# Attention and a feed-forward layer on one core: a third room for the values' parts, row sums inverted on 128 rows, and new beats for a unit's work

## The chip, the cores and the metric

The kernel runs on one core of one Trainium2 chip. The metric is the device time of one execution in microseconds (us). PE is TensorE, DVE is VectorE, ACT is ScalarE, POOL is GpSimd and SP the engine that issues most of the DMAs. The runs of the kernel before took 746.44 to 747.60 us, median 746.81.

## The reference

Attention of 4 batches and 8 heads over 576 positions with head dimension 64, with a bias from a small network on the positions' distance, followed by a feed-forward layer over the 2304 tokens:

```python
scores = scale * np.matmul(q, k.transpose(0, 1, 3, 2)) + bias
scores = scores - np.max(scores, axis=-1, keepdims=True)
attn = np.exp(scores)
attn = attn / (np.sum(attn, axis=-1, keepdims=True) + 1e-09)
x = np.matmul(attn, v)                 # per head, then heads side by side: (2304, 512)
h = x @ w_in                           # (2304, 2048)
g = 0 if h <= -1, h if h >= 1, else (h + 1) ** 2 / 4
out = g @ w_out                        # (2304, 512)
```

## The kernel before

The program has three stages. The first (to about 68 us) makes the bias and writes it to DRAM. The second (about 68 to 342 us) is the attention, the third the feed-forward layer. The change lies in the second.

**Precision.** Matrix products run on values that are split in a high part (a cast to fp32r) and a low part (the value minus the high part). So each operand takes a cast and a subtraction, and each product takes two or three matmuls.

**A unit.** The attention is cut into 16 units, n = 0 to 15: a pair of heads p = n // 4 and a batch b = n % 4. The 576 query rows of two heads are five blocks of 128 rows: k = 0 to 3 hold 128 rows of either head (j = 0, 1), and "L" holds the last 64 rows of both. The steps of a unit have short names:

- S0 to S3, SL (`score`, matmuls of L431 into tiles S): scores in PSUM, in the two rooms of pool `psS`. A block takes both rooms, so the next block starts when the maxima before it have read their room.
- m00 to m31, mL (`maxima`, L457 on DVE): adds the bias, writes the tile e to SBUF and the row's extreme to mx.
- x00 to x31, xL (`exps`, L454 on ACT): the exponential, in place, with the row sum into a column of `sum` (128 x 9).
- T00 to T31, TL, Ts0, Ts1 (`transpose...`, L434 on PE): e transposed into PSUM tiles T, in the four rooms of pool `psT`, which the output tiles O share. Ts1 also transposes `sum` into 9 x 128 of its tile.
- h.. and l.. (`high`, `low_`): split the transposed tile into hi and lo. For four keys in the set POOL, ACT copies the tile to SBUF (L533, tile c) and POOL makes hi (L541) and lo (L542). For the others ACT casts hi (L536) and DVE subtracts for lo (L544).
- O00h, O00l, ... O11l (`values`, L431, tiles O): hi and lo times the values' tile vs. c00 to c11 (L569 on ACT) copy the result out, and `store` sends it to DRAM (L577 on SP).
- R (`sums_out`): ACT adds 1e-9 to the transposed sums and writes r, 9 x 128 (L548). r (`inverse`): DVE inverts it (L552) and SP stores it in rT (L553). The feed-forward stage multiplies by it.
- kh, kl0, kl1, vh, vl: the split of the next unit's inputs. kh (L171) casts queries and keys on DVE, vh (L179) casts the values into the front half of vs on DVE, and POOL subtracts for the back halves (L147). vs has two rooms, so vh of unit n+1 must wait until the last matmul on vs of unit n-1, O11l.

**The order.** Nothing is scheduled at run time: every engine takes its instructions in program order. The table BEAT gives each step of a unit a time in us from its S0, and units lie UNIT = 15.5 apart. All events of all units are sorted by that time and written out in that order. A unit's last steps (beats over 15.5) so fall into the next unit. XQ and WQ put extra work into some units: the split of the feed-forward stage's first inputs x (units 4, 8, 12 to 15) and of its first weights (units 6, 7, 9, 10).

Of the kernel before, what the change touches and what calls it, by code (L numbers as in the profile page):

```python
# [8 lines left out]
F32 = mybir.dt.float32  # L9
F32R = mybir.dt.float32r  # L10
I32 = mybir.dt.int32
U16 = mybir.dt.uint16
AF = mybir.ActivationFunctionType
ALU = mybir.AluOpType
# [7 lines left out]
P = 128  # L22
NP = H // 2
HS = S // 2
NG = S // 16
# [4 lines left out]

CBW = (1, 1, 32, C, C, C * H, S // 4, NG)
CB = sum(CBW)
CFG = dict(un=[('paaa', 'paav')[g in (1, 30, 32, 34)] for g in range(NG)], bb=5, mv=1, rb='a', pool=((0, 0), (0, 1), (1, 1), (2, 0)), sb=4, keep=1, drain=2, diag='a', rb2='v', eps='v', rc=2, rbb=1, hb=2, rawb=(2, 2), eb=4, seq=0, pb=(6, 9, 12, 14, 16), pq=22, tb=6, ub=12, low0='ppp', anch=(8, 8, 16, 23, 23), low1='ppp', ob=4, gb=4, fin=2, sbf=('v', 'v', 'v', 'v', 'v'), bsE=(), ytail='p')
EPS = 1e-9
RB = 2
FIRST = ((0, 3), (1, 5), (2, 33))
XQ = {(0, 0): (39, "raw", 4, 12.4), (1, 0): (80, "raw", 8, 12.4), (2, 0): (118, "raw", 12, 12.4), (3, 0): (139, "bias", 15, 6.3),
      (0, 1): (125, "x", 13, 12.4), (1, 1): (131, "raw", 14, 12.4), (2, 1): (144, "x", 15, 9.7), (3, 1): (151, "raw", 15, 12.4)}
WQ = {(0, 0): (52, 6), (0, 1): (70, 7), (1, 0): (91, 9), (1, 1): (100, 10)}
LB = ((1, 1), (2, 1), (3, 2), (3, 3), (2, 3))  # L40
UNIT = 15.5
BEAT = {
# [10 lines left out]
}  # L53
POOL, SB, KEEP, RBB = CFG["pool"], CFG["sb"], CFG["keep"], CFG["rbb"]
BIG = 3.0e38
# [4 lines left out]
def attn_cpb_moe_kernel(ctx, tc, qk, vL, cb, win, wout, lw, ident, ii, out):  # L60
    nc = tc.nc
# [16 lines left out]
    wp0 = ctx.enter_context(tc.tile_pool(name="m_w0", bufs=1))  # L78
    rps = [ctx.enter_context(tc.tile_pool(name="m_raw", bufs=1))]
    loads = ExitStack()  # L80
    lp = ctx.enter_context(tc.tile_pool(name="a_load", side="right", bufs=2))
    bp = loads.enter_context(tc.tile_pool(name="a_bias", side="right", bufs=CFG["bb"]))
    qp = loads.enter_context(tc.tile_pool(name="a_qkv", side="right", bufs=2))
# [4 lines left out]
    last_y, stored = [], []  # L88
    half_s = wp0.tile([P, 1], F32, name="half_s")
    nc.gpsimd.memset(half_s, 0.5)  # L90
    eps_s = wp0.tile([P, 1], F32, name="eps_s")
    nc.gpsimd.memset(eps_s, EPS)
    floor_s = wp0.tile([P, 1], F32, name="floor_s")
    nc.gpsimd.memset(floor_s, -4095.5 / 8192)

# [44 lines left out]
    qkv, bias = {}, {}  # L140
    go = [False]

    def low(o, i, h, x="p"):
        if x == "v":
            nc.vector.tensor_tensor(out=o, in0=i, in1=h.bitcast(F32), op=ALU.subtract)
            return
        pool(nc.gpsimd.tensor_tensor(out=o, in0=i, in1=h.bitcast(F32), op=ALU.subtract))  # L147

    def keep(ins):
        tc.keep_in_program_order(ins)  # L150
# [9 lines left out]
    def prep(n):  # L160

        L = CFG["low0"] if n == 0 else CFG["low1"] if n == 1 else "ppp"
        a = qkv[n] = {}

        def high(ins):
            keep(ins)

        def high_k():

            a["h"] = qp.tile([P, KQ], F32R, tag="kh", name=f"kh{n}", bufs=CFG["hb"])  # L170
            high(nc.vector.tensor_copy(a["h"], a["r"]))  # L171

        def load_r():
            a["r"] = lp.tile([P, KQ], F32, tag="qk", name=f"qk{n}", bufs=CFG["rawb"][0])
            nc.sync.dma_start(out=a["r"], in_=qk[n])

        def high_v():
            a["v"] = qp.tile([P, 10, P], F32R, tag="vs", name=f"vs{n}")
            high(nc.vector.tensor_copy(a["v"][:, :, 0:D], a["rv"]))  # L179

        def load_v():
            a["rv"] = lp.tile([P, 10, D], F32, tag="v", name=f"v{n}", bufs=CFG["rawb"][1])
            nc.sync.dma_start(out=a["rv"].rearrange("p a b -> p (a b)"), in_=vL[n])

        def part(i):


            def f():
                if i == 0:
                    a["l"] = qp.tile([P, KQ], F32R, tag="kl", name=f"ls{n}")  # L190
                c = slice(KW * i, KW * i + (QW if i else KW))
                low(a["l"][:, c], a["r"][:, c], a["h"][:, c], L[i])

            return f

        def v_():
            low(a["v"][:, :, D:P], a["rv"], a["v"][:, :, 0:D], L[2])

        return [load_r, load_v, high_k, high_v, part(0), part(1), v_]

    preps = {0: prep(0), 1: prep(1)}


    with ExitStack() as ph:
# [21 lines left out]
        diag = [ac.tile([P, P], F32, name=f"diag{i}") for i in range(2)]  # L226
# [9 lines left out]
        pq = cp.tile([P, 2, C, H], F32, name="pq")  # L236
# [148 lines left out]
    def split_x(k, j, home):  # L385

        r, rr = load_x(0, k, j, home)
        x = r[:, 0]

        def add():  # L390
            keep(nc.vector.tensor_tensor(out=x, in0=x, in1=r[:, 1], op=ALU.add))

        def scaled():
            keep(nc.vector.tensor_tensor(out=x, in0=x, in1=rr, op=ALU.mult))

        def high():
            xs[k, j] = [x_tile(j, k, i, f"x{'hl'[i]}0_{k}_{j}") for i in range(2)]
            keep(nc.scalar.copy(xs[k, j][0], x))

        def rest():  # L400
            h, l = xs[k, j]
            pool(nc.gpsimd.tensor_tensor(out=l, in0=x, in1=h.bitcast(F32), op=ALU.subtract))

        return add, scaled, high, rest

    with ExitStack() as ph:
# [3 lines left out]
        sp = ph.enter_context(tc.tile_pool(name="a_small", bufs=2))  # L410
# [32 lines left out]
        def on(n, t, f, *a):  # L443
            events.append((UNIT * n + t, len(events), f, a))

        def unit(n):
            p, b = n // B, n % B
            q = qkv[n]
            e, sc, tr, out, mx = {}, {}, {}, {}, {}
            eT = {}  # L450
            sm = stp.tile([P, 9], F32, tag="sum", name=f"sum{n}", bufs=3)
# [86 lines left out]
            def low_(key):  # L538
# [4 lines left out]
                else:  # L543
                    keep(nc.vector.tensor_tensor(out=lo, in0=ps, in1=hi.bitcast(F32), op=ALU.subtract))  # L544

            def sums_out():
                r = out["r"] = sp.tile([9, P], F32, tag="r", name=f"r{n}")
                keep(nc.scalar.activation(r, out["sum"], AF.Identity, bias=eps_s[:9]))  # L548

            def inverse():  # L550
                r = out["r"]
                keep(nc.vector.reciprocal(out=r, in_=r))  # L552
                nc.sync.dma_start(out=rT[p][b].rearrange("(k q) -> k q", q=P), in_=r)  # L553

            def values(half, j, part):
# [43 lines left out]
            for x in ("L", "s0", "s1"):  # L599
                at(f"h{x}", high, x)  # L600
                at(f"l{x}", low_, x)
            at("R", sums_out)
            at("r", inverse)
            for half in range(2):
# [20 lines left out]
                on(B * (p - 1) + b, 3.1 * k_ + 0.5, load_b)  # L625

        def plan_x(k, j):
            T, home, n, t = XQ[k, j]
            fs = []

            def load():
                assert all((k, t_) in made for t_ in range(TH * j, TH * j + TH))
                fs.extend(split_x(k, j, home))

            on(T // 10, T % 10 * UNIT / 10, load)
            for i, dt in enumerate((0, 0.9, 2.4, 3.4)):
                on(n, t + dt, lambda i=i: fs[i]())

        for kj in XQ:
            plan_x(*kj)  # L640
        for fo, (T, n) in WQ.items():
            load, *fs = weight_ahead(*fo, rps[0])
            on(T // 10, T % 10 * UNIT / 10, load)
            for t, f in zip((7.0, 9.3, 12.4, 13.3, 15.8), fs):
                on(n, t, f)
        go[0] = True
        while events:
            i = min(range(len(events)), key=lambda i: events[i][:2])
            _, _, f, a = events.pop(i)
# [5 lines left out]
    with ExitStack() as ph:  # L655
# [220 lines left out]
        for k in range(2):  # L876
            t = T1 + 1 + 12 * k
# [17 lines left out]
        for blk in (0, TB):  # L895
            for m in range(2 * NF):
                f, j = m // 2, m % 2
# [50 lines left out]
        for g in range(NG2):  # L948
            blk, f = b2, 2 * g
            for s_ in range(NS):  # L950
                t = NS * g + s_
# [30 lines left out]
                else:  # L982
                    fo, j = {2: (f, 0), 4: (f + 1, 1), 5: (f + 1, 0), 6: (f, 1)}[s_]
# [80 lines left out]
```

## Time and profile before

| | |
|---|---|
| median of the runs | 746.81 us |
| the profiled execution | 745.66 us, its span 743.5 us |
| PE busy | 704.1 us, 95% of the span |
| DVE, ACT, POOL busy | 513.3, 513.6 and 512.3 us, 69% each |
| mean granted TensorE clock | 0.993 of full speed |

A busy share of PE is not a measure of its work: matmuls overlap, and their ends are modelled. What PE loses is read from the starts of its instructions. The engines' waits name what released them. Times in the rows count from the span's start.

### The profile page before, as it was taken

The page shows a single profiled execution, that of the slowest core. Times are in us where ns is not written, and L with a number is a line of the kernel's source. Part 1 is how long each engine was busy: PE and PEld are TensorE (multiplying, and loading weights), DVE is VectorE, ACT ScalarE, POOL GpSimd, SP SyncE. Part 2 cuts the span into 40 slices and gives each one's busy share as a digit, 9 for nine tenths or more (in the row PEclk, how much of TensorE's full clock was granted, in tenths as well). Part 3 has the DMA queues.
Part 4 walks back from the last instruction along what each step waited for, and adds up shares of the span by engine and source line. Part 5 has one row for each costly group of instructions (what it writes and reads, how often), then busy time and mean ns, then how long its engine had stood idle before and what let it go on. Part 6 is the DMA issues. An engine that isn't in the chain of part 4 may idle for free.

```text
span 743.5 us, 14025 instructions
## 1 busy us (share of the span) xinstructions
PE 704.1 (95%) x4864; PEld 603.9 (81%) x4864; DVE 513.3 (69%) x993; ACT 513.6 (69%) x1124; POOL 512.3 (69%) x445
## 2 busy tenths in 40 slices
PE   5777999999999999999999999999999999999997
PEld 2234888888888888888989889898999988888896
DVE  7998767778887877896876766354455556666653
ACT  8996887889989888796565656444534447666563
POOL 7984777787887878885667677466555645666652
PEclk9998999999999999999999999999999999999999
DMA  6788334633753454326445554132021002000002
GB/s 191 237 283 254 113 118 151 199 131 114 221 158 124 145 177 128 87 70 191 130 161 163 188 151 143 45 92 78 1 64 33 1 1 85 1 2 1 0 1 85
DMA packets 51237, 83.97 MB, mean 113 GB/s; under 512 B 11216, under 2 KB 31456, under 8 KB 51168
## 3 DMA queue, kind: packets, MB, share of 16 engines
q1 hardware_dynamic: 50880, 82.87, 35.8%
q8 instruction: 38, 0.62, 0.4%
q14 instruction: 31, 0.25, 0.1%
q10 hardware_dynamic: 288, 0.22, 0.1%
HBM read 57.95 MB, written 25.12 MB: 112 GB/s over the span
## 4 chain that ended last, share of the span: by engine, by line
PE 55%; ACT 10%; DVE 8%; POOL 7%; issue 6%; DMA 4%; SPq 1%; DVEq 0%; POOLq 0%; ACTq 0%
PE y L672 23%; PE h L672 15%; PE p L672 7%; PE O L431 4%; PE S L431 3%; POOL lo L542 3%; ACT e L454 2%; DVE e L457 2%; PE T L434 2%; ACT hi L536 2%; POOL ls L147 2%; POOL hi L541 1%; DMA bias<-bias_d 1%; DVE r L552 1%; DMA x<-rT 1%
## 5 line engine op out<-in xcount | busy, mean ns | idle before, releaser
L914 POOL TENSOR_TENSOR gl<-c,gh 128x384 fp32r<-128x384 f32 x64 | 70.6, 1103 | 101.9 <-issue 87.3
L454 ACT ACTIVATE e<-e,mx 128x576 f32<-128x576 f32 x128 | 99.1, 775 | 36.3 <-DVE mx L457 36.0
L672 PE MATMUL y<-w1h,gl 128*128 128x512 f32 x288 | 114.0, 396 | 0.0
L672 PE MATMUL y<-w1l,gh 128*128 128x512 f32 x288 | 113.7, 395 | 0.0
L672 PE MATMUL y<-w1h,gh 128*128 128x512 f32 x288 | 112.0, 389 | 0.0
L457 DVE CUSTOM_DVE_ANT_0 e<-S,bias 128x576 f32<-128x576 f32 x128 | 90.8, 744 | 8.5 <-PE S L431 5.6
L542 POOL TENSOR_TENSOR lo<-c,hi 128x512 fp32r<-128x512 f32 x64 | 83.6, 1307 | 5.1
L541 POOL CAST hi<-c 128x512 fp32r<-128x512 f32 x64 | 48.4, 757 | 56.1 <-ACT c L533 56.1
L732 ACT ACTIVATE c<-c,half_s 128x384 f32<-128x384 f32 x64 | 39.4, 616 | 61.6 <-DVE c L729 61.5
L434 PE MATMUL T<-id_s,e 128*128 128x128 f32 x512 | 74.4, 279 | 0.0
L938 POOL TENSOR_TENSOR gl<-c,gh 128x384 fp32r<-128x384 f32 x32 | 32.7, 1023 | 47.8 <-issue 22.3
L434 PEld LDWEIGHTS T<-id_s,e 128*128 128x128 f32 x512 | 59.3, 144 | 6.5 <-issue 3.2
L672 PEld LDWEIGHTS y<-w1h,gl 128*128 128x128 f32 x288 | 54.0, 187 | 11.5
L672 PEld LDWEIGHTS y<-w1l,gh 128*128 128x128 f32 x288 | 54.0, 187 | 8.0
L270 ACT ACTIVATE u<-lw,nthr 128x576 f16<-128x576 f32 (+17 forms) x104 | 57.5, 644 | 4.2 <-DVE lw L235 2.4
L672 PEld LDWEIGHTS y<-w1h,gh 128*128 128x128 f32 x288 | 54.1, 188 | 7.7
L431 PE MATMUL O<-hi,vs 128*128 128x256 f32 (+1 forms) x320 | 58.5, 313 | 0.0
L289 PEld LDWEIGHTS <-qh 128*32 128x32 f16 x704 | 19.5, 101 | 47.7 <-issue 23.0
L272 POOL TENSOR_SCALAR u<-lw,thr 128x576 f16<-128x576 f32 (+17 forms) x36 | 51.7, 1453 | 7.6 <-DVE lw L235 3.9
L431 PE MATMUL S<-kh 64*128 64x288 f32 x256 | 53.3, 349 | 3.7 <-DVE mx L457 2.2
L431 PE MATMUL O<-lo,vs 128*128 128x256 f32 (+1 forms) x320 | 54.4, 300 | 0.0
L910 ACT CAST gh<-c 128x384 fp32r<-128x384 f32 x64 | 32.8, 513 | 30.3 <-DVE c L735 28.5
(263 smaller groups left out, 2043.9 us busy)
## 6 DMA issues: line engine op xcount, KB each, us to landing
bias_d<-y SPq DMA_DIRECT2D x36, 295.5 KB, 5.0
qk<-in_qk_dram SPq DMA_DIRECT2D x16, 640.0 KB, 4.1
x<-xT SPq DMA_DIRECT2D x48, 192.0 KB, 3.4
raw<-in_win_dram SPq DMA_DIRECT2D x16, 512.0 KB, 4.5
raw<-in_wout_dram SPq DMA_DIRECT2D x16, 512.0 KB, 3.5
v<-in_vL_dram SPq DMA_DIRECT2D x16, 320.0 KB, 5.5
bias<-bias_d SPq DMA_DIRECT2D x16, 288.0 KB, 3.7
out_dram<-o SPq DMA_DIRECT2D x17, 256.0 KB, 2.1
```

The source lines that it names most:

```text
L270: tc.keep_in_program_order(nc.scalar.activation(u[:, :n_], lw1[:, :n_], AF.Sigmoid, bias=nthr[:, m : m + 1], scale=STEEP))
L272: EN[x].tensor_scalar(out=u[:, :n_], in0=lw1[:, :n_], scalar1=thr[:, m : m + 1], scalar2=None, op0=ALU.is_gt)
L431: keep(nc.tensor.matmul(*a, **k))
L434: keep(nc.tensor.transpose(*a))
L454: keep(nc.scalar.activation(ev, ev, AF.Exp, bias=m, scale=-1.0, accum_out=sm[:, at : at + 1]))
L457: keep(nc.vector.tensor_tensor_reduce(out=o.rearrange("p (a b) -> p a b", a=2), in0=ps[:, :, :HS], in1=of.rearrange("p (a b) -> p a b", a= ...
L541: keep(nc.gpsimd.tensor_copy(hi, ps))
L542: keep(nc.gpsimd.tensor_tensor(out=lo, in0=ps, in1=hi.bitcast(F32), op=ALU.subtract))
L672: a = nc.tensor.matmul(out, w, x, start=start, stop=stop)
L732: keep(nc.scalar.activation(c, c, AF.Square, scale=0.5, bias=half_s))
L910: keep(nc.scalar.copy(gh, c))
L914: keep(nc.gpsimd.tensor_tensor(out=gl, in0=c, in1=gh.bitcast(F32), op=ALU.subtract))
```

## The change

Four things are changed.

1. The tile vs gets three rooms instead of two.
2. The row sums are inverted before the transposition. DVE adds 1e-9 to `sum` (128 x 9) and inverts it there; Ts1 transposes the inverses, and ACT only copies them out to r, from where SP stores them.
3. In the set POOL the key (1,1) is replaced by (3,1), so l11 is now made by DVE and the parts of (3,1) by POOL.
4. The table of beats is new, and so are some places of the extra work. Weights now fall into units 6, 7, 10 and 11.

```diff
-CFG = dict(..., pool=((0, 0), (0, 1), (1, 1), (2, 0)), ...)
+CFG = dict(..., pool=((0, 0), (0, 1), (2, 0), (3, 1)), ...)
...
-WQ = {(0, 0): (52, 6), (0, 1): (70, 7), (1, 0): (91, 9), (1, 1): (100, 10)}
+WQ = {(0, 0): (53, 6), (0, 1): (70, 7), (1, 0): (93, 10), (1, 1): (110, 11)}
...
-    "h30": 14.3, "O00l": 14.5, "l21": 14.8, "T31": 15.1, "xL": 15.3, "l30": 15.4, "diag": 16.1, "c00": 16.6,
+    "T30": 15.07, "xL": 15.09, "c00": 15.89, "r": 15.97, "diag": 16.17, "h31": 16.68, "TL": 16.69,
...
-            a["v"] = qp.tile([P, 10, P], F32R, tag="vs", name=f"vs{n}")
+            a["v"] = qp.tile([P, 10, P], F32R, tag="vs", name=f"vs{n}", bufs=3)
...
+            def inverse():
+                keep(nc.vector.tensor_scalar(out=sm, in0=sm, scalar1=EPS, scalar2=None, op0=ALU.add))
+                keep(nc.vector.reciprocal(out=sm, in_=sm))
+
             def sums_out():
-                r = out["r"] = sp.tile([9, P], F32, tag="r", name=f"r{n}")
-                keep(nc.scalar.activation(r, out["sum"], AF.Identity, bias=eps_s[:9]))
-
-            def inverse():
-                r = out["r"]
-                keep(nc.vector.reciprocal(out=r, in_=r))
+                r = sp.tile([9, P], F32, tag="r", name=f"r{n}")
+                keep(nc.scalar.copy(r, out["sum"]))
                 nc.sync.dma_start(out=rT[p][b].rearrange("(k q) -> k q", q=P), in_=r)
...
-            for t, f in zip((7.0, 9.3, 12.4, 13.3, 15.8), fs):
+            for t, f in zip((6.85, 11.0, 13.1, 15.4, 17.9), fs):
                 on(n, t, f)
```

What this does to the order is seen at two places. The first is DVE in the middle of unit 10. In a name such as lo10_0_4125 the first number is the unit and the next the half or block; the last is a buffer. T10_1_1 is the transposed tile of step T11, S10_3_0 the scores of S3 for head 0, vs11 the values' tile of the next unit. Before:

```order
L544 TENSOR_TENSOR lo9_1_3985<-T9_s1_4113,hi9_1_3984 128x320
L171 CAST kh11_4147<-qk11_3866 128x1280
L552 RECIPROCAL r9_4138<-r9_4138 9x128
L457 ISA e10_2_4150,mx10_2_4149<-S10_2_0_4151,bias2_2_3373 128x576
L457 ISA mx10_2_4149 128x1
L457 ISA e10_2_4150,mx10_2_4149<-S10_2_1_4152,bias2_2_3373 128x576
L457 ISA mx10_2_4149 128x1
L544 TENSOR_TENSOR lo10_0_4125<-T10_1_0_4171,hi10_0_4124 128x4x128
L179 CAST vs11_4220<-v11_4070 128x10x64
L457 ISA e10_3_4201,mx10_3_4200<-S10_3_0_4202,bias2_3_3434 128x576
L457 ISA mx10_3_4200 128x1
L457 ISA e10_3_4201,mx10_3_4200<-S10_3_1_4203,bias2_3_3434 128x576
```

The same stretch after:

```order
L544 TENSOR_TENSOR lo9_1_3981<-T9_s1_4113,hi9_1_3980 128x320
L171 CAST kh11_4149<-qk11_3873 128x1280
L457 ISA e10_2_4153,mx10_2_4152<-S10_2_0_4154,bias2_2_3380 128x576
L457 ISA mx10_2_4152 128x1
L457 ISA e10_2_4153,mx10_2_4152<-S10_2_1_4155,bias2_2_3380 128x576
L457 ISA mx10_2_4152 128x1
L544 TENSOR_TENSOR lo10_0_4126<-T10_1_0_4171,hi10_0_4125 128x4x128
L179 CAST vs11_4218<-v11_4071 128x10x64
L544 TENSOR_TENSOR lo10_0_4126<-T10_1_1_4187,hi10_0_4125 128x4x128
L457 ISA e10_3_4201,mx10_3_4200<-S10_3_0_4202,bias2_3_3437 128x576
L457 ISA mx10_3_4200 128x1
L544 TENSOR_TENSOR lo10_0_4126<-T10_s0_4196,hi10_0_4125 128x256
```

The inversion of r is gone from ahead of m20; the cast of vs11 keeps its place behind l10, but l11 now stands between it and m30, and ls0 between m30 and m31. The inversion now stands ahead of the next unit's m00, behind l21 (and, in this unit, a weight's cast):

```order
L544 TENSOR_TENSOR lo10_1_4242<-T10_2_1_4253,hi10_1_4241 128x4x128
L132 CAST w0h1_1483<-a10_4234 128x512
L547 TENSOR_SCALAR sum10_4039<-sum10_4039 128x9
L548 RECIPROCAL sum10_4039<-sum10_4039 128x9
L457 ISA e11_0_4304,mx11_0_4303<-S11_0_0_4305,bias2_0_2804 128x576
```

The second place is ACT where the sums of unit 9 leave the transposed tile T9_s1, with the semaphores that an instruction waits for. Before:

```order
L536 CAST hi9_1_3984<-T9_s1_4113 128x320 [waits PE_49]
L454 ACTIVATE e10_1_4089,sum10_4039<-e10_1_4089,mx10_1_4088 128x576 [waits DVE_49]
L548 ACTIVATE r9_4138<-T9_s1_4113,eps_s_113 9x128 [waits DMAHW5_49]
L454 ACTIVATE e10_1_4089,sum10_4039<-e10_1_4089,mx10_1_4088 128x576 [waits DVE_49]
L533 COPY c4_4166<-T10_0_0_4119 128x512 [waits PE_49,Pool_49]
```

After:

```order
L536 CAST hi9_1_3980<-T9_s1_4113 128x320 [waits PE_49]
L454 ACTIVATE e10_1_4091,sum10_4039<-e10_1_4091,mx10_1_4090 128x576 [waits DVE_49]
L552 COPY r9_4146<-T9_s1_4113 9x128 [waits DMAHW5_49,DVE_49]
L454 ACTIVATE e10_1_4091,sum10_4039<-e10_1_4091,mx10_1_4090 128x576
L116 ACTIVATE raw10_3871<-raw10_3871,floor_s_113 128x512 [waits DMAHW1_49]
```

The step stands where it stood, but now it waits for DVE (for ls1, which reads the same tile and is written ahead of it); before, ls1 was written behind it and waited for it.

## Rows read from the trace of the kernel before

**Rows 1.** The page: span; busy us, share of the span and instructions by engine.
```profile
span 743.5 us, 14025 instructions
...
PE 704.1 (95%) x4864; PEld 603.9 (81%) x4864; DVE 513.3 (69%) x993; ACT 513.6 (69%) x1124; POOL 512.3 (69%) x445
```
**Rows 2.** Windows: stretch, length; busy PE, PEld, DVE, ACT, POOL; clock, DMA share, GB/s.
```profile
220.00:260.00 40.00, 38.82 (x335) 34.22 (x334) 32.48 (x72) 36.63 (x92) 31.98 (x28) 1.00 0.43 137
260.00:300.00 40.00, 38.04 (x317) 33.09 (x316) 29.88 (x70) 32.87 (x84) 32.22 (x29) 1.00 0.47 143
460.00:500.00 40.00, 40.00 (x201) 36.07 (x200) 18.22 (x29) 17.11 (x31) 24.34 (x21) 1.00 0.18 58
```
**Rows 3.** Waits, 100 to 335 us: who waited for whom, total us, times, longest.
```profile
DVE vs L179 <- PE O L431: 28.6, 13, 2.2
ACT e L454 <- DVE mx L457: 27.5, 23, 2.0
```
**Rows 4.** Timeline of PE: start us, us, what, [idle before]; SL of unit 0.
```profile
80.09 0.40 PE L431 MATMUL S_L<-kh 128*128 128x288 f32 x1
```
**Rows 5.** Timeline of PE around SL of units 6, 7 and 15; S1, S2, S3 of unit 7.
```profile
179.33 1.04 PE L434 MATMUL T<-id_s,e 128*128 128x128 f32 x8
180.84 0.37 PE L431 MATMUL S_L<-kh 128*128 128x288 f32 x1 [0.48 <-DVE mx L457]
...
181.86 0.63 PE L434 MATMUL T<-id_s,e 128*128 128x128 f32 x4
...
186.81 0.40 PE L431 MATMUL S<-kh 64*128 64x288 f32 x2
...
187.81 0.44 PE L434 MATMUL T_s<-id_s,e 128*128 128x128 f32 x2
...
191.07 0.66 PE L434 MATMUL T<-id_s,e 128*128 128x128 f32 x4
...
193.04 0.86 PE L431 MATMUL S<-kh 64*128 64x288 f32 x2
...
194.49 1.00 PE L431 MATMUL O<-hi,vs 128*128 128x320 f32 x5
...
196.06 1.03 PE L434 MATMUL T<-id_s,e 128*128 128x128 f32 x8
197.58 0.37 PE L431 MATMUL S_L<-kh 128*128 128x288 f32 x1 [0.48 <-DVE mx L457]
...
331.71 1.04 PE L434 MATMUL T<-id_s,e 128*128 128x128 f32 x8
332.50 0.38 PE L431 MATMUL S_L<-kh 128*128 128x288 f32 x1
...
333.38 0.60 PE L434 MATMUL T<-id_s,e 128*128 128x128 f32 x4
```
**Rows 6.** Timeline of DVE in unit 7: ls1 of unit 6, inversion, m20, l10, vh.
```profile
190.08 0.49 DVE L544 TENSOR_TENSOR lo<-T_s,hi 128x320 fp32r<-128x320 f32 x1 [0.72 <-ACT r L548]
...
191.22 0.93 DVE L552 RECIPROCAL r<-r 9x128 f32<-9x128 f32 x1
192.08 0.68 DVE L457 CUSTOM_DVE_ANT_0 e<-S,bias 128x576 f32<-128x576 f32 x1
...
193.38 0.67 DVE L544 TENSOR_TENSOR lo<-T,hi 128x512 fp32r<-128x512 f32 x1
196.26 0.49 DVE L179 CAST vs<-v 128x640 fp32r<-128x640 f32 x1 [2.21 <-PE O L431]
```
**Rows 7.** Timeline of POOL in unit 15.
```profile
332.02 1.29 POOL L542 TENSOR_TENSOR lo<-c,hi 128x512 fp32r<-128x512 f32 x1
```
**Rows 8.** Timeline of DVE in units 0 and 15.
```profile
78.69 0.67 DVE L179 CAST vs<-v 128x640 fp32r<-128x640 f32 x1
...
329.63 0.54 DVE L391 TENSOR_TENSOR x<-x 128x384 f32<-128x384 f32 x1
...
332.40 1.32 DVE L391 TENSOR_TENSOR x<-x 128x384 f32<-128x384 f32 x1
```

More of the change, by code (lines that the diff above doesn't have):

```diff
@@ L32 @@
 CB = sum(CBW)
-CFG = dict(un=[('paaa', 'paav')[g in (1, 30, 32, 34)] for g in range(NG)], bb=5, mv=1, rb='a', pool=((0, 0), (0, 1), (1, 1), (2, 0)), sb=4, keep=1, drain=2, diag='a', rb2='v', eps='v', rc=2, rbb=1, hb=2, rawb=(2, 2), eb=4, seq=0, pb=(6, 9, 12, 14, 16), pq=22, tb=6, ub=12, low0='ppp', anch=(8, 8, 16, 23, 23), low1='ppp', ob=4, gb=4, fin=2, sbf=('v', 'v', 'v', 'v', 'v'), bsE=(), ytail='p')
+CFG = dict(un=[('paaa', 'paav')[g in (1, 30, 32, 34)] for g in range(NG)], bb=5, mv=1, rb='a', pool=((0, 0), (0, 1), (2, 0), (3, 1)), sb=4, keep=1, drain=2, diag='a', rb2='v', eps='v', rc=2, rbb=1, hb=2, rawb=(2, 2), eb=4, seq=0, pb=(6, 9, 12, 14, 16), pq=22, tb=6, ub=12, low0='ppp', anch=(8, 8, 16, 23, 23), low1='ppp', ob=4, gb=4, fin=2, sbf=('v', 'v', 'v', 'v', 'v'), bsE=(), ytail='p')
 EPS = 1e-9
@@ L36 @@
 FIRST = ((0, 3), (1, 5), (2, 33))
-XQ = {(0, 0): (39, "raw", 4, 12.4), (1, 0): (80, "raw", 8, 12.4), (2, 0): (118, "raw", 12, 12.4), (3, 0): (139, "bias", 15, 6.3),
-      (0, 1): (125, "x", 13, 12.4), (1, 1): (131, "raw", 14, 12.4), (2, 1): (144, "x", 15, 9.7), (3, 1): (151, "raw", 15, 12.4)}
-WQ = {(0, 0): (52, 6), (0, 1): (70, 7), (1, 0): (91, 9), (1, 1): (100, 10)}
+USUAL = (10.0, 13.1, 14.05, 17.9)
+XQ = {(0, 0): (39, "raw", 4, USUAL), (1, 0): (80, "raw", 8, USUAL), (2, 0): (120, "raw", 12, USUAL), (3, 0): (140, "bias", 15, (6.1, 6.2, 8.0, 8.1)),
+      (0, 1): (125, "x", 13, USUAL), (1, 1): (133, "raw", 14, USUAL), (2, 1): (144, "x", 15, (9.5, 10.0, 10.9, 11.1)), (3, 1): (153, "raw", 15, (13.1, 13.2, 14.5, 16.3))}
+WQ = {(0, 0): (53, 6), (0, 1): (70, 7), (1, 0): (93, 10), (1, 1): (110, 11)}
 LB = ((1, 1), (2, 1), (3, 2), (3, 3), (2, 3))
@@ L90, in attn_cpb_moe_kernel @@
     nc.gpsimd.memset(half_s, 0.5)
-    eps_s = wp0.tile([P, 1], F32, name="eps_s")
-    nc.gpsimd.memset(eps_s, EPS)
     floor_s = wp0.tile([P, 1], F32, name="floor_s")
@@ L627, in plan_x @@
         def plan_x(k, j):
-            T, home, n, t = XQ[k, j]
+            T, home, n, ts = XQ[k, j]
             fs = []
@@ L635, in plan_x @@
             on(T // 10, T % 10 * UNIT / 10, load)
-            for i, dt in enumerate((0, 0.9, 2.4, 3.4)):
-                on(n, t + dt, lambda i=i: fs[i]())
+            for i, t in enumerate(ts):
+                on(n, t, lambda i=i: fs[i]())
         for kj in XQ:
```

19 rows, old and new, of the table BEAT are left out of this document.

## The prediction, written before the result was known

> **What bounds the kernel now.** I read the page first, then the windows, then PE's timeline inside a unit, then DVE's. The page gives PE as busy for 95% of the span [rows 1], which says little by itself. The windows divide the kernel: in the feed-forward stage PE is busy for all of 40.00 us [rows 2], and nothing of that stage's own work is changed. So the attention is what can move. There PE's busy time is 38.04 to 38.82 us of 40, with every other engine below 37 [rows 2].
>
> How much PE loses is read from its starts. SL of unit 0 starts at 80.09 and SL of unit 15 at 332.50 [rows 4, 5]: 252.41 us for 15 units. A plain unit takes 197.58 - 180.84 = 16.74 us [rows 5]. Fifteen of those are 251.1; the other 1.3 us I put down to units that carry extra work.
>
> Two stalls lie in each unit. The first is before SL: in unit 6 eight transposes start at 179.33 and SL follows at 180.84, 1.51 us later; in unit 15, where SL does not wait, the same step takes 332.50 - 331.71 = 0.79. That is 0.72, and SL itself then takes 1.02 (to 181.86) against 0.88 (to 333.38), 0.14 more [rows 5]. The second is in S3: it takes 194.49 - 193.04 = 1.45 us, S1 takes 1.00 [rows 5], so 0.45. Together 1.31 us per unit. Without them PE needs 16.74 - 1.31 = 15.43 us for a unit.
>
> DVE shows where the stalls come from. Vh of the next unit waits 2.21 us for PE's last O matmul, and only then m30 runs, for which SL waits [rows 6]. This is one of 13 such waits, 28.6 us in total; ACT's waits for maxima, 27.5 us, are the shadow of it [rows 3]. Earlier in the unit ls1 waits 0.72 us for ACT's r, and the inversion takes 0.93 right before m20 [rows 6]; S3 waits for m20 and m21.
>
> **The third room.** With three rooms, vh of unit n+1 takes the room of unit n-2, whose last reader lies a whole unit back. The 2.21 us go. What is late next for SL? From S3's end PE has O11h and O11l (196.06 - 194.49 = 1.57) and eight transposes (0.79), so 2.36 us to SL's start, in another order but the same work [rows 5]. In that time DVE must finish m30. It starts it when S3 is done, if vh and l11 are done by then. Counted from S2's end (191.07): m20 and m21 are 1.36, l10 0.67, vh 0.49, l11 0.67, so 3.19 us; S3 ends 2.97 us after S2's end (1.97 to its start, 1.00 to run) [rows 5, 6]. So m30 starts about 0.3 us after S3 and takes 0.68: SL's need is met some 1.4 us early. l11 also needs ACT's cast of T11, which stands behind an exponential and an output copy; that may cost some tenths of the 1.4 us, not all.
>
> **The inversion.** Ahead of m20 the inversion (0.93) and ls1's wait (0.72) go, and m20 starts when S2 ends. PE has 193.04 - 191.07 = 1.97 us from S2's end to S3's start [rows 5]; m20 and m21 take 1.36 [rows 6]. S3 does not wait, by 0.6 us. The price: two operations on 128 x 9 on DVE, not in the trace; the inversion of 9 x 128 bounds them at 0.93 each from above [rows 6], nothing from below; with an eighth or less of the free elements I take 0.1 each. They stand ahead of the next unit's m00 and wait for the last exponential on ACT, which is the new coupling: behind them are m00, m01 and so S1. SL to the end of the next S0 is about 4 us of PE work, mL and the exponential after it need under 2, so I cost the wait at nothing; if ACT is late by more than that cover, it is paid in full at S1.
>
> ACT's copy of r now waits for DVE's ls1, at most its 0.49 us [rows 6]. Queued behind it on ACT are x11 and the copies of T00 and T01, which POOL waits for. The other direction of this wait cost DVE 0.72; ACT has the time as long as it is not the bound.
>
> **The other engines at 15.4 us a unit.** From 260 to 300 us ACT is busy 32.87 of 40, 13.7 us of a unit of 16.74; from 220 to 260, with two weights in it, 36.63, or 15.3 [rows 2]. POOL's 32.22 make 13.5, DVE's 32.48 make 13.6. So all fit in 15.4, ACT in units with a weight only just. Moving (1,1) to DVE and (3,1) to POOL changes no engine's count. I allow 0.2 us in each of the four units with a weight.
>
> **DMAs.** Their share is 0.43 and 0.47 [rows 2] and grows by 8%. Stores and loads keep their queue; the store of r comes from ACT's copy rather than DVE's inversion, about a microsecond earlier. Nothing of this is costed.
>
> **The sum.** PE's floor is 15.43; for the transposes that now stand apart I take 15.5. 15 x 15.5 = 232.5, plus 1.3 for the extra work as before, plus 4 x 0.2: 234.6 against 252.41, a gain of 17.8 us. PE's order up to SL of unit 0 is the same, and after SL of unit 15 PE runs its tail and the saturated stage with the same work: nothing there, with 1 us either way. The profiled execution took 745.66 and gives 727.9; the median of the runs lies 1.15 above it (746.81), so I expect **729.0 us**. The least: fifteen units at 15.43 and nothing for weights or extra work, a gain of 21 us, 726.
>
> **Rival 1: POOL holds vh up.** In unit 15 DVE's addition at 332.40 takes 1.32 us, the same at 329.63 takes 0.54; POOL's subtraction runs from 332.02 to 333.31, and the addition ends 0.41 us after that [rows 7, 8]. So DVE is held until POOL's instruction is done. In unit 0 vh takes 0.67 rather than 0.49 [rows 6, 8]. In the new order vh stands where POOL works through l00, kl0 and kl1 without a pause, and the wait could reach a POOL instruction's 1.29. Vh, l11 and m30 then slip by that: it eats 1.1 to 1.4 us of cover. With l11's wait for ACT on top some 0.4 us per unit come out at SL: 6 us, 735. The Trainium skill states this as a rule ("SBUF — State Buffer", section "SBUF: two separate sides"): VectorE and GpSimd share a pair of ports, an exclusive lock that is held for a whole instruction, while the other blocks; the rows above agree, and by that rule the place of vh beside POOL's back-to-back work is the weak point of this change.
>
> **Rival 2: SL's wait only changes its cause.** m30 now stands behind l11, which waits for ACT's cast behind x20 and c10. If ACT runs late by 1.4 us, SL waits 0.86 as before, and only S3's 0.45 and its like are won: 17.8 - 15 x 0.86 = 4.9, 742.
>
> **Rival 3, slower: ACT becomes the bound.** ACT has 13.7 us of work and now three waits in a unit in which all that follows is queued: r for DVE, the last exponential's maximum, the first one's. If these add up to over 3.0 us, a unit takes more than 16.74. At 3.4 us, 15 x 0.4 = 6 us lost: 753. Against it: ACT's waits for maxima came to 27.5 us over 14 units, 2 us each [rows 3], and their main cause goes.
>
> **Rival 4: it doesn't do what it says.** A DMA (the values' load, which waits for POOL's part of vs) takes the place of the room as what vh waits for, and the period stays near 16.7: 746. The DMA shares speak against it.
>
> **How the numbers follow.** Forecast (725.5 to 733) 0.63; rival 1, 0.15; rival 2, 0.07; rival 3, 0.08; rival 4, 0.04; below 725.5, 0.03. The range is 725.5 to 738: from the floor to beyond rival 1, with some of what lies between it and rival 2. Left out are rivals 2 to 4 and the lower end, 0.2. A change of 0.2% (1.5 us) is about what a measurement of this kernel can tell from none: faster 0.63 + 0.15 + 0.07 + 0.03 = 0.88, the same 0.04, slower 0.08.
>
> **What would show it.** In the profile after, SL to SL should be 15.4 to 15.6 us, with no idle time named DVE mx before SL; the wait of vs for O should be gone, ls1 should follow m11 without one. PE's 252.41 us from SL of unit 0 to SL of unit 15 should be about 235, and what follows SL of unit 15 as long as before (411 us to the span's end). Rival 1 shows as vh taking 1 us and more and SL waiting for mx; rival 2 as DVE's lo waiting for ACT's hi before m30; rival 3 as ACT without idle time and m00 late behind the inversion. The prediction is wrong if the period stays over 16.2.

## The result, and the profile after

The changed kernel takes 736.66 us (734.78 to 736.93), the kernel before beside it 747.2 us: a ratio of 0.985, 95% interval 0.983 to 0.987. It is faster by 10.5 us. That is inside the predicted range, but the forecast of 729.0 us promised 17.8, and its own band (725.5 to 733) was missed. The profiled execution took 736.86 us.

The page of the changed kernel, span and busy time, answers [rows 1]: PE's busy time falls by 9 us with the span, DVE's grows by 17.

```profile
span 734.5 us, 14012 instructions
...
PE 695.0 (95%) x4864; PEld 600.4 (82%) x4864; DVE 530.4 (72%) x1009; ACT 512.4 (70%) x1124; POOL 514.0 (70%) x444
```

The windows, for [rows 2] (length; PE, PEld, DVE, ACT, POOL; clock, DMA share, GB/s):

```profile
220.00:260.00 40.00, 40.00 (x360) 36.64 (x360) 34.10 (x79) 38.36 (x98) 35.56 (x31) 1.00 0.49 150
260.00:300.00 40.00, 37.27 (x322) 32.54 (x319) 37.10 (x71) 33.66 (x86) 32.37 (x29) 1.00 0.44 134
460.00:500.00 40.00, 40.00 (x201) 36.11 (x201) 19.20 (x30) 16.94 (x31) 23.24 (x20) 1.00 0.23 75
```

From 220 to 260 us PE is now without a gap in the attention, as in the saturated stage. From 260 to 300 it is worse off than before (37.27 against 38.04), and there DVE's 37.10 is 7.2 us more than before. So the change did in one stretch what was forecast and in another the opposite.

The waits, 100 to 335 us, for [rows 3]: the wait of vs for O is gone, ACT's wait for maxima has fallen from 27.5 to 10.5 us.

```profile
ACT e L454 <- DVE mx L457: 10.5, 16, 1.1
```

The timeline of PE answers [rows 4, 5]: start, duration, what, idle before it. SL of units 0, 4, 5, 6, 7 and 15, and in between what waits in unit 4 (T21 before SL, the two first matmuls of S1 of unit 5 after it).

```profile
80.11 0.40 PE L431 MATMUL S_L<-kh 128*128 128x288 f32 x1 [0.97 <-DVE mx L457]
...
141.56 0.63 PE L434 MATMUL T<-id_s,e 128*128 128x128 f32 x4 [0.18 <-DVE lo L544]
142.14 0.40 PE L431 MATMUL S_L<-kh 128*128 128x288 f32 x1
...
148.90 0.40 PE L431 MATMUL S<-kh 64*128 64x288 f32 x1 [0.61 <-DVE mx L457]
149.58 0.40 PE L431 MATMUL S<-kh 64*128 64x288 f32 x1 [0.28 <-DVE mx L457]
...
159.16 0.38 PE L431 MATMUL S_L<-kh 128*128 128x288 f32 x1
...
174.53 0.38 PE L431 MATMUL S_L<-kh 128*128 128x288 f32 x1
...
189.88 0.38 PE L431 MATMUL S_L<-kh 128*128 128x288 f32 x1
...
322.45 0.40 PE L431 MATMUL S_L<-kh 128*128 128x288 f32 x1
```

A plain unit takes 174.53 - 159.16 = 15.37 us, and 189.88 - 174.53 = 15.35 with a weight in it, against 16.74 before. But from SL of unit 4 to SL of unit 5 it is 159.16 - 142.14 = 17.02. From SL of unit 0 to SL of unit 15 it is 242.34 us (before 252.41). Fifteen units at 15.36 would be 230.4: 11.9 us lie elsewhere. They lie around units 4, 8 and 12 to 15 alone: 2.2, 2.5 and 7.2 us. These are the units in which DVE does the x work, the part of the extra work that adds the two halves of a block of the attention's result (x, line 391) and scales it by the inverted sums (line 394). There are eight such blocks.

The timeline of DVE in unit 3 (the first line, a plain place) and unit 4:

```profile
129.08 1.27 DVE L547 TENSOR_SCALAR sum<-sum 128x9 f32<-128x9 f32 x1
...
138.29 0.69 DVE L179 CAST vs<-v 128x640 fp32r<-128x640 f32 x1
138.91 1.91 DVE L391 TENSOR_TENSOR x<-x 128x384 f32<-128x384 f32 x1
140.74 0.68 DVE L544 TENSOR_TENSOR lo<-T,hi 128x512 fp32r<-128x512 f32 x1
...
143.02 1.56 DVE L394 TENSOR_TENSOR x<-x,xr 128x384 f32<-128x384 f32 x1
...
146.41 1.57 DVE L547 TENSOR_SCALAR sum<-sum 128x9 f32<-128x9 f32 x1
148.01 0.22 DVE L548 RECIPROCAL sum<-sum 128x9 f32<-128x9 f32 x1
```

The timeline of POOL beside it:

```profile
138.59 3.64 POOL L147 TENSOR_TENSOR ls<-qk,kh 128x640 fp32r<-128x640 f32 x2
...
142.87 1.29 POOL L542 TENSOR_TENSOR lo<-c,hi 128x512 fp32r<-128x512 f32 x1
...
146.38 1.57 POOL L147 TENSOR_TENSOR vs<-v,vs 128x640 fp32r<-128x640 f32 x1
```

Read the two together. The addition to x took 0.54 us where it stood free [rows 8]; here it takes 1.91 and starts 0.32 us into POOL's work on kl. The scale starts 0.15 us into POOL's lo and takes 1.56. The 1e-9 on 128 x 9, nine elements a row, starts 0.03 us into POOL's vl and takes 1.57 us. T21 then waits for l11, which stands behind the addition (140.74, done at 141.42), and S1 waits for the maxima behind the inversion. In plain units the 1e-9 takes 1.27 us as well, and PE doesn't notice: unit 1 lasts 15.37 us with 1.27, unit 2 15.35 with 0.17.

One wait of PE for maxima is left before SL, in unit 0 (the first line of PE's timeline): 0.97 us. There the cast vh stands beside POOL's kl and takes 1.57 us:

```profile
77.22 1.57 DVE L179 CAST vs<-v 128x640 fp32r<-128x640 f32 x1
```

```profile
76.87 3.31 POOL L147 TENSOR_TENSOR ls<-qk,kh 128x640 fp32r<-128x640 f32 x2
```

SL of unit 0 starts at 80.11 all the same, against 80.09 before.

The costs over the attention (60 to 345 us), DVE grouped by line (count, busy us, mean ns, idle before):

```profile
L547 DVE TENSOR_SCALAR sum<-sum 128x9 f32<-128x9 f32 x16 | 14.2, 886 | 1.1 <-ACT e_L L454 0.3
...
L391 DVE TENSOR_TENSOR x<-x 128x384 f32<-128x384 f32 x8 | 11.9, 1483 | 0.0
L179 DVE CAST vs<-v 128x640 fp32r<-128x640 f32 x15 | 11.8, 789 | 0.0
...
L394 DVE TENSOR_TENSOR x<-x,xr 128x384 f32<-128x384 f32 x5 | 7.7, 1546 | 0.0
```

In the kernel before, the addition had a mean of 705 ns, the scale (these five) of 931. The same work costs 2.1 and 1.7 times as much.

My theory then, A: DVE's operations from SBUF to SBUF are held while POOL's instruction runs, and the new beats put the x work beside POOL's kl and lo, where PE has no cover left. The rivals: it is the amount of the x work (B); the third room or the new inversion, not the beats, makes what gain there is (told apart by doing each alone).

### The profile page after: what moved, and what is told of

It reads as the page before. It is cut to its first block, busy times and chain, and to the rows that moved or that the text cites. A ratio compares the mean times of both kernels' runs of the same rounds, so it can differ in the third digit from the quotient of the medians.

```text
span 734.5 us, 14012 instructions
## 1 busy us (share of the span) xinstructions
PE 695.0 (95%) x4864; PEld 600.4 (82%) x4864; DVE 530.4 (72%) x1009; ACT 512.4 (70%) x1124; POOL 514.0 (70%) x444
## 4 chain that ended last, share of the span: by engine, by line
PE 60%; DVE 11%; POOL 6%; ACT 5%; issue 4%; DMA 3%; SPq 2%; DVEq 0%; POOLq 0%; ACTq 0%
PE y L672 21%; PE h L672 13%; PE p L672 7%; PE O L431 6%; PE S L431 5%; PE T L434 4%; DVE e L457 3%; POOL lo L542 2%; DMA x<-rT 1%; DVE x L394 1%; DVE lo L544 1%; SPq L377 1%; DVE sum L547 1%; PE T_s L434 1%; PE S_L L431 1%
## 5 line engine op out<-in xcount | busy, mean ns | idle before, releaser
L542 POOL TENSOR_TENSOR lo<-c,hi 128x512 fp32r<-128x512 f32 x64 | 85.2, 1331 | 5.1
L541 POOL CAST hi<-c 128x512 fp32r<-128x512 f32 x64 | 44.1, 689 | 43.0 <-ACT c L533 42.9
L431 PE MATMUL O<-hi,vs 128*128 128x256 f32 (+1 forms) x320 | 57.0, 308 | 0.3 <-ACT x L569 0.3
L431 PE MATMUL S<-kh 64*128 64x288 f32 x256 | 49.4, 346 | 6.5 <-DVE mx L457 5.6
L729 DVE TENSOR_SCALAR c<-h 128x384 f32<-128x384 f32 x64 | 35.4, 552 | 27.2 <-PE h L672 25.4
```

The source lines that it names most:

```text
L431: keep(nc.tensor.matmul(*a, **k))
L541: keep(nc.gpsimd.tensor_copy(hi, ps))
L542: keep(nc.gpsimd.tensor_tensor(out=lo, in0=ps, in1=hi.bitcast(F32), op=ALU.subtract))
L729: keep(nc.vector.tensor_scalar(out=c, in0=h, scalar1=-1.0, scalar2=1.0, op0=ALU.max, op1=ALU.min))
```

## The experiments

**The third room alone.** The kernel before with one edit.

```diff
-            a["v"] = qp.tile([P, 10, P], F32R, tag="vs", name=f"vs{n}")
+            a["v"] = qp.tile([P, 10, P], F32R, tag="vs", name=f"vs{n}", bufs=3)
```

> The kernel before with the third room for vs alone. Theory (the stall before SL comes from the cast of the values waiting for PE, the stall in S3 from the inversion and from ls1's wait): the 0.86 us before SL go in every unit, the 0.45 us in S3 stay, so a plain unit takes 15.9 us instead of 16.74 and the time is about 747 - 13 = 734 us. Rival (the room alone does nothing with the old beats, since m30 then waits for something else): a plain unit of 16.5 us or more, 744 us or more.

Measured: 731.67 us, ratio 0.980 (0.976 to 0.985). All units take 15.78 to 15.87 us, those with x work too; only the last takes 16.05. One line of the change does at least as well as the whole: the two intervals of the ratio overlap a little, but the fifteen units take 237.55 us against 242.34. What is left of the stalls shows in PE's timeline of this kernel, around S3 of unit 8:

```profile
202.91 0.86 PE L431 MATMUL S<-kh 64*128 64x288 f32 x2
...
204.36 0.99 PE L431 MATMUL O<-hi,vs 128*128 128x320 f32 x5
...
205.92 1.04 PE L434 MATMUL T<-id_s,e 128*128 128x128 f32 x8
206.71 0.38 PE L431 MATMUL S_L<-kh 128*128 128x288 f32 x1
```

S3 still takes 204.36 - 202.91 = 1.45 us, to the hundredth what it took before [rows 5]; eight transposes to SL take 206.71 - 205.92 = 0.79, what they take without a wait. So the room took away the stall before SL (0.86) and left the one in S3 (0.45). And vh is held by POOL here:

```profile
L179 DVE CAST vs<-v 128x640 fp32r<-128x640 f32 x15 | 18.0, 1202 | 0.0
```

1.20 us in the mean, against 0.51 before, and SL does not wait for it. The scale of x takes 1.53 to 1.54 us in five units here, as long as in the changed kernel, and these units are no longer than the others. So an operation that is held need not cost anything; that hangs on what stands behind it.

**All of the change but the third room.**

```diff
-            a["v"] = qp.tile([P, 10, P], F32R, tag="vs", name=f"vs{n}", bufs=3)
+            a["v"] = qp.tile([P, 10, P], F32R, tag="vs", name=f"vs{n}")
```

> The changed kernel with two rooms for vs. Theory: the cast of vs waits for O11l again, and l11 and m30 stand behind it; O11l's end to m30's end is then 0.1 + 0.5 + 0.7 + 0.7 = 2.0 us, of which PE covers 0.4 with T21: a stall of 1.6 us before SL, a plain unit of 17.0 instead of 15.36 us, 737 + 24 = 761 us. Rival (the beats do it, the room is a detail): a plain unit under 15.7 us, under 742 us.

Measured: 769.43 us, ratio 1.031 (1.028 to 1.034), units of 17.05 to 17.3 us up to the first x work, as expected (17.0), then of 17.8 to 19.5, and 16.2 for the last. The direction is as expected and the size larger; where the rest comes from was not followed. The new beats are no use without the room.

**The new inversion without the 1e-9** (that addition is left out; a row's sum is far above it).

```diff
-                keep(nc.vector.tensor_scalar(out=sm, in0=sm, scalar1=EPS, scalar2=None, op0=ALU.add))
```

> The changed kernel without the addition of 1e-9 to the row sums (left out; the inversion stays). Theory A (the addition, SBUF to SBUF on DVE, is held 1.3 to 1.5 us by POOL's subtraction for vs, and the inversion is not of that kind): the inversion runs at once in about 0.2 us, m00 comes over 1 us earlier in the units with x work, and the 0.9 us before and in S1 go in five of them: about 732 us. Theory B (POOL holds whichever of the two comes first): the inversion takes 1.5 us instead, and the time stays at 736 to 737 us.

Measured: 732.76 us, ratio 0.982 (0.979 to 0.985); SL of unit 0 to SL of unit 15 237.68 us, 4.7 less than with it. Plain units stay at 15.36; units with x work take 15.8 to 16.9. DVE's timeline of this kernel, the inversion alone:

```profile
289.27 0.21 DVE L547 RECIPROCAL sum<-sum 128x9 f32<-128x9 f32 x1
```

And POOL's at that time:

```profile
289.20 1.56 POOL L147 TENSOR_TENSOR vs<-v,vs 128x640 fp32r<-128x640 f32 x1
```

The same 128 x 9 elements, at the same place in the order, beside the same instruction of POOL: the addition of a constant was held for 1.51 us in the changed kernel (1.57 in unit 4), the inversion is not held at all. So theory A is too wide as it stands: not every operation from SBUF to SBUF is held. Why the one is and the other isn't, no run here shows.

**The changed kernel without DVE's x work** (the addition and the scale of the eight blocks are left out).

```diff
-            keep(nc.vector.tensor_tensor(out=x, in0=x, in1=r[:, 1], op=ALU.add))
+            pass
...
-            keep(nc.vector.tensor_tensor(out=x, in0=x, in1=rr, op=ALU.mult))
+            pass
```

> The changed kernel without the two DVE operations (addition and scaling) on the eight blocks of x in the attention (left out; loads, ACT's cast and POOL's subtraction stay). Theory A (these two, with two SBUF operands, are held by POOL and push m30, m31, mL and the inversion): the units with x work fall from 15.9 to 17.6 us to about 15.4, and the 242.3 us from SL of unit 0 to SL of unit 15 to about 231: 726 us. Theory B (the later units are held by POOL's own extra subtraction or by a DMA for x): less than half of it goes, over 731 us.

Measured: 724.4 us, ratio 0.971 (0.968 to 0.973), 231.46 us for the fifteen units, or 15.43 each. The x work is what 10.9 of the 11.9 us are tied to. The rest lies in the same units (15.43 to 15.73 us), where POOL still makes the low part of x and the 1e-9 takes 0.97 to 1.27 us. The run does not say yet whether it is the amount of the x work or its place.

**The x work elsewhere.** Nothing is left out. POOL sat idle from 133.76 to 136.66 us in the changed kernel, some 7.5 us after SL; the addition and the scale of five blocks go there, for three of them one unit later, and the loads of two weights, which use the same room, follow. In `XQ` a block has the time of its load, its room, its unit, and the beats of its four steps (addition, scale, high part on ACT, low part on POOL). Three of the blocks (QUIET) have ACT's and POOL's steps moved as well, two (LATE) only DVE's.

```diff
-USUAL = (10.0, 13.1, 14.05, 17.9)
-XQ = {(0, 0): (39, "raw", 4, USUAL), (1, 0): (80, "raw", 8, USUAL), (2, 0): (120, "raw", 12, USUAL), ...
-      (0, 1): (125, "x", 13, USUAL), (1, 1): (133, "raw", 14, USUAL), ...
+QUIET, LATE = (6.1, 6.2, 8.0, 8.1), (6.1, 6.2, 14.05, 17.9)
+XQ = {(0, 0): (39, "raw", 5, QUIET), (1, 0): (80, "raw", 9, QUIET), (2, 0): (120, "raw", 13, QUIET), ...
+      (0, 1): (125, "x", 13, LATE), (1, 1): (137, "raw", 14, LATE), ...
```

> The changed kernel with nothing left out; the add and the scale of five of the eight x blocks are put some 6 beats after a unit's first scores, where GpSimd sits idle in the trace of the changed kernel (2.9 us of it at 133.8 us), three of the blocks one unit later for it. Theory A (these operations cost their place beside GpSimd's, not their work): the add takes 0.55 us and the scale 0.6 to 0.9 in place of 1.91 and 1.55, the units that now hold them stand at 15.4 to 15.6 us, unit 15 and its neighbours keep one to two us, and the time is 726 to 729 us. Theory B (their amount of work is what a unit can't hold, wherever it stands): the units that hold them go to 16.2 to 17 us as they did, and the time stays within 734 to 738.

Measured: 727.77 us, ratio 0.975 (0.973 to 0.978). Units 1 to 12 take 15.35 to 15.42 us, whether they hold x work or not; the fifteen units 233.03. DVE's timeline of unit 5:

```profile
151.66 0.55 DVE L391 TENSOR_TENSOR x<-x 128x384 f32<-128x384 f32 x1
152.24 0.56 DVE L394 TENSOR_TENSOR x<-x,xr 128x384 f32<-128x384 f32 x1
```

POOL's, before and after them:

```profile
148.69 1.29 POOL L542 TENSOR_TENSOR lo<-c,hi 128x512 fp32r<-128x512 f32 x1
154.06 1.01 POOL L402 TENSOR_TENSOR xl<-x,xh 128x384 fp32r<-128x384 f32 x1 [4.08 <-ACT xh L398]
```

0.55 and 0.56 us instead of 1.91 and 1.56, with POOL idle. In units 5 and 9 theory A holds and B falls: the work is the same, the place was the cost. (The old place was both beside POOL's work and ahead of l11; whether the operations would cost there without being held, no run separates.) That it was POOL's own step for x that cost before is ruled out by the run above, which left that step where it was.

What is left is in the last units: 16.13 and 16.88 us from SL of unit 12 to that of 14. There three of the five blocks stand, two of them at one place:

```profile
274.63 1.02 DVE L391 TENSOR_TENSOR x<-x 128x384 f32<-128x384 f32 x2
...
276.51 0.75 DVE L457 CUSTOM_DVE_ANT_0 e<-S,bias 128x576 f32<-128x576 f32 x1
```

POOL is idle there (273.19 to 277.03) and none of the four operations is held, yet together they take 1.9 us ahead of m20, and S3 takes 1.67 us instead of 1.00. At this one place the amount does cost, as theory B has it. In the next unit S3 waits behind one block and a kh of 1.64 us.

**The same without the 1e-9** (left out).

> The same with the 1e-9 on the row sums left out as well. Theory A: with the x operations out of GpSimd's way the 1.27 us of the 1e-9 is covered as in plain units, so that leaving it out adds under 2 us: 725 to 728 us. Theory C (the 1e-9 operation costs by itself, whatever else is there): 3 to 5 us under the kernel that keeps it.

Measured: 728.11 us, the fifteen units 232.97. No difference (727.77 with it). The 4.7 us that its removal gave above were a toll of the two delays together: held alone it is covered, as in plain units (or nearly: without DVE's x work a unit with a 1e-9 of 1.27 us took 15.73); behind a held x operation it is not.

**The old inversion in the new order.** The changed kernel, with ACT's copy adding the 1e-9 and DVE inverting r on 9 x 128 as before.

```diff
-                keep(nc.vector.tensor_scalar(out=sm, in0=sm, scalar1=EPS, scalar2=None, op0=ALU.add))
-                keep(nc.vector.reciprocal(out=sm, in_=sm))
...
-                keep(nc.scalar.copy(r, out["sum"]))
+                keep(nc.scalar.activation(r, out["sum"], AF.Identity, bias=eps_s[:9]))
...
+                keep(nc.vector.reciprocal(out=r, in_=r))
...
-    "r": 15.97
+    "r": 23.3
```

> The changed kernel with one part undone: the row sums are inverted as before, ScalarE copies the 9x128 transposed sums with the 1e-9 as its bias, VectorE inverts them there, nine rows long, some 2 beats later. Theory A (the cost of the changed kernel's units with x work is its VectorE operations that go from SBUF to SBUF while GpSimd's run, the 1e-9 on 128x9 among them): without that operation the units stand as in the kernel that left the 1e-9 out, plain ones at 15.36 to 15.5 us, those with x work at 15.8 to 16.9, and the time is 732 to 735 us: the new form of the inversion is worth nothing or less. Theory B (the inversion on 128 rows is what brought the plain unit from 15.8 to 15.36 us, since VectorE no longer waits for ScalarE's copy): plain units go back to 15.7 to 15.8 and the time is 739 us or more.

Measured: 738.05 us, ratio 0.988 (0.985 to 0.991); plain units 15.8 to 16.1. That is near what theory B expected (15.7 to 15.8 us, 739 or more) and far from A, but the place chosen was bad. DVE's timeline of this kernel (its lines are two higher) shows why, in unit 11:

```profile
250.20 1.79 DVE L173 CAST kh<-qk 128x1280 fp32r<-128x1280 f32 x1
251.91 0.74 DVE L459 CUSTOM_DVE_ANT_0 e<-S,bias 128x576 f32<-128x576 f32 x1
...
252.59 0.94 DVE L554 RECIPROCAL r<-r 9x128 f32<-9x128 f32 x1
253.46 0.68 DVE L459 CUSTOM_DVE_ANT_0 e<-S,bias 128x576 f32<-128x576 f32 x1
```

The inversion parts the two maxima of S2, and S3 waits for the second of them. (Here kh is held too; in plain units it takes 0.82 us, and S3 still 1.40.) The plain units of 16.1 us are those with vh at 1.85 us; with 0.49 it is 15.8. So the inversion was tried once more, at "r": 29.1, where DVE had been idle for 1.1 us before mL, the maxima of SL.

> The kernel with the old inversion once more, its reciprocal on 9x128 (0.94 us) moved 5.8 beats later, to where VectorE sat idle for 1.1 us before SL's softmax. Theory A (the old inversion costs only where it stands: at its former beat it lay between S2's two softmaxes, and S3 waited for the second): plain units 15.36 to 15.5 us, the time 732 to 735 us. Theory B (the 128-row form itself is what brought the plain units down, by the ACT copy and the wait that it takes off): plain units stay at 15.8 to 16.1 and the time at 737 us or more.

Measured: 740.22 us, ratio 0.992 (0.989 to 0.994). Theory A is half right: plain units take 15.38 to 15.45, so the form of the inversion is not what makes a plain unit short; but the time is above its 732 to 735 us. Units with a weight now take 16.0 to 16.8 (the longer ones hold an addition of x too), and those with x work up to 17.6. In unit 10 SL starts at 239.34 and mL, behind a weight's step (239.81, 1.07 us) and the inversion (240.80, 0.93), at 241.66, 2.3 us later; in the plain unit 3 of the changed kernel the lag is 1.1. The old form thus has no free place among those two; no other was tried.

**Room and new inversion, with the beats of before.** The third room, the two lines of the new inversion at "r": 16.0, nothing else.

> The kernel before with the third room and the 128-row inversion, all other beats as before. In the kernel with the third room alone all units stood at 15.8 us, and VectorE waited 0.7 us in each for ScalarE's copy of the sums. Theory A (the new beats brought the plain unit from 15.8 to 15.36 us, the inversion does no more than move its own work): units at 15.7 to 15.9 us, the time 730 to 734 us. Theory B (the inversion did, through that wait): units at 15.4 to 15.5 us, the time 725 to 727 us, the fastest so far.

Measured: 728.15 us, ratio 0.976 (0.972 to 0.979), not to be told from the kernel with the x work moved. Counted from SL to SL, units come in two kinds. The plain units 1, 2, 3, 5 and 11 take 15.39 to 15.40 us; unit 0 and those with extra work take 15.73 to 15.79 (one takes 16.93, with S1 waiting twice for mx). The plain ones have lost S3's 0.45 us: the inversion no longer stands ahead of m20. The others have a new loss in S1 or S0. PE's timeline: the S1 that follows SL of a plain unit (1) and of one with x work (8), 5.82 and 5.81 us after it, and between them the S0 that follows SL of a unit with a weight (7):

```profile
102.88 0.40 PE L431 MATMUL S<-kh 64*128 64x288 f32 x2
...
194.37 0.73 PE L431 MATMUL S<-kh 64*128 64x288 f32 x2
...
212.93 0.77 PE L431 MATMUL S<-kh 64*128 64x288 f32 x2
```

DVE's after SL of unit 1:

```profile
98.14 0.76 DVE L457 CUSTOM_DVE_ANT_0 e_L<-S_L,biasL 128x576 f32<-128x576 f32 x1 [1.55 <-PE S_L L431]
...
100.09 1.04 DVE L547 TENSOR_SCALAR sum<-sum 128x9 f32<-128x9 f32 x1
...
106.00 0.49 DVE L544 TENSOR_TENSOR lo<-T_s,hi 128x320 fp32r<-128x320 f32 x1 [0.57 <-ACT r L552]
```

And after SL of units 7 and 8:

```profile
195.78 0.16 DVE L547 TENSOR_SCALAR sum<-sum 128x9 f32<-128x9 f32 x1
...
206.56 1.15 DVE L391 TENSOR_TENSOR x<-x 128x384 f32<-128x384 f32 x1
...
208.52 0.74 DVE L457 CUSTOM_DVE_ANT_0 e_L<-S_L,biasL 128x576 f32<-128x576 f32 x1
...
210.54 1.16 DVE L547 TENSOR_SCALAR sum<-sum 128x9 f32<-128x9 f32 x1
...
212.49 0.75 DVE L457 CUSTOM_DVE_ANT_0 e<-S,bias 128x576 f32<-128x576 f32 x1
```

After SL of unit 8 the pair of matmuls is stretched to 0.77 us; the second of the maxima, m01, ends at 213.24, and PE's next pair starts at 213.31. The 1e-9 is held in the plain unit as well (1.04 us), and there S1 does not wait. What differs is mostly the start of mL: 1.40 us after SL here, behind the x work, and 1.08 in the plain unit. After SL of unit 7 the 1e-9 isn't held at all (0.16), and S0 is stretched. So the new loss goes with the extra work ahead of mL, and the held 1e-9 is at most a part of it.

Theory B holds for plain units: with the old beats they take 15.39 us, with the new ones 15.36, so the new beats are not what makes a plain unit short. Taken with the run above (plain units of 15.38 to 15.45 with the old form), what matters is neither the form of the inversion nor the beats around it, but that no inversion stands ahead of either of the maxima of S2. And it is the inversion alone: ls1 still waits 0.57 us for ACT's r here, and S3 does not wait.

## Why the prediction was right or wrong, point by point

**What bounds the kernel: right.** The floor was put at 15.43 us. Plain units take 15.35 to 15.37, a little under it. PE's 40.00 of 40 us from 220 to 260 says the same.

**The two stalls and their causes: right, and now shown one by one.** The prediction gave the room SL's 0.86 us and the inversion S3's 0.45. The third room alone brought 16.74 to 15.8 and left S3 at 1.45; the inversion on top of it brought plain units to 15.39, and S3's wait went. The wait of ls1, which the prediction named beside the inversion, had no part in S3's. That SL has cover once the room is there is shown as well: with the room alone vh took 1.20 us, over twice its time, and SL did not wait. Of the signs named beforehand, the wait of vs and that of ls1 are gone, but in unit 0 an idle time named DVE mx is left before SL. The period stays under 16.2, by little if all fifteen units are meant: 242.34 / 15 = 16.16.

**The price of the inversion: the step that failed first.** It was "two operations on 128 x 9", bounded by 0.93 each, taken at 0.1. The inversion itself takes 0.22, inside the bounds. The 1e-9 takes 0.89 in the mean and up to 1.57, over the upper bound, because the bound came from an instruction that wasn't held. "Behind them are m00, m01 and so S1" named the right victims, but the delay was looked for in ACT's lateness, and it came from POOL. The cover held it in plain units. In units with x work it did not, and with the x work moved it costs nothing again.

**The extra work: the term that was mis-sized.** It was carried over as 1.3 us "as before", with 0.2 for each unit with a weight, 2.1 us in all. Measured: 11.9 us, all of it around x work; units with a weight alone stay at 15.35. The working counted what operations the change moves on DVE and what they took in the old place, not what POOL does in the new. Plain units came 0.14 us better than 15.5, or 2.1 in fifteen; so the fifteen units took 242.34 rather than 234.6. The remaining 7.7 us are the miss in the attention. Another 1.05 came after SL of unit 15 (412.05 us to the span's end against 411.0, just over the 1 us allowed). With the x work moved to where POOL is idle the fifteen units take 233.03 and the kernel 727.8 us, by 1.6 and 1.2 under the forecast: the rest of the sum stands. So the step that failed is the overlap on DVE: operations were carried over at their old price into places beside POOL's instructions.

**Rival 1 had the mechanism at the wrong instruction, and the range holds by luck in part.** Its 735 us lies nearest to the result, and the range reached beyond 733 only to take it in; what filled that part of the range was another instruction. It looked for a DVE operation held by POOL at vh, in every unit, 0.4 us each. Vh was held (0.79 us in the mean, 1.20 with the old beats) and cost nothing that plain units show; only in unit 0 did SL wait behind it. The x operations and the 1e-9 were held, in six units that lost 11.9 us; 9.3 of these went when the x work was moved. The rule that it cited, from the Trainium skill ("SBUF — State Buffer", section "SBUF: two separate sides"), was wide enough: it gives the exclusive lock to DVE operations with two SBUF inputs (against a POOL operation that reads SBUF) as well as to those in a two-port mode, and the addition and the scale of x are of the first kind. The traces agree: 0.55 us with POOL idle, 1.91 and 1.56 beside its instructions; the subtractions with one input in PSUM stayed at 0.69 beside the same ones. The rows for it were in front of me [rows 7, 8], for an addition to x of all things; I moved the conclusion to vh and left x at its old price.

**The other rivals.** DVE's lo waits for ACT's hi for 7.9 us in all between 100 and 335 us, and plain units show no stall at SL: rival 2 did not come about. ACT is busy 38.36 of 40 us from 220 to 260 while PE has no gap, so rival 3 didn't either, though with 4% to spare. The wait of vs is gone, which ends rival 4.

## What to carry to other kernels

When a change moves work of VectorE, price each moved operation by what GpSimd runs at the new place: here the same addition cost 0.55 or 1.91 us, and whether the delay counts depends on how much cover PE's consumer has behind it. Do the parts of a compound change one at a time: one line (a third buffer) was worth 14.5 us, and the new inversion some 2 to 4 us on top (1.8 in the fifteen units; the intervals of the time overlap). The reordering around them made the kernel some 7 to 8.5 us slower than these two alone (736.66 against 728.15, by the ratios 0.985 against 0.976), until ten small operations were moved, most of them into gaps of GpSimd's: 727.8 us, 18.5 under the kernel before beside it, and no better than the third buffer and the inversion with the old order.

## What the runs showed of the hardware

An addition of a constant to 128 x 9 elements from SBUF to SBUF took 0.17 us free and 1.57 beside a POOL instruction that ran for as long; RECIPROCAL on the same tile took 0.20 to 0.22 us in all its instances, beside such an instruction too (0.21). Inverting 9 rows of 128 took 0.93 us, 128 rows of 9 took 0.22. Of the casts, kh took 0.82 us free and up to 1.81 held (old inversion in the new order), and vh 0.49 and up to 1.86 (unit 0 of the kernel with the x work moved).
